# Attention stage of a three-layer kernel: causal blocks cut in half, 64 by 64 tiles, two tile forms per pair

## The chip, the cores and the metric

One Trainium2 chip, one core. The metric is the device time of one execution in microseconds. The median of three runs of the kernel before is 829.82 us (828.93 to 831.88).

## What is computed

A retention layer (attention without softmax, with a causal decay) on 4 batches of 8 heads, 576 positions, head size 64, and behind it two dense layers with a hidden width of 2,048 on 2,304 tokens of width 512.

```python
scores = scale * np.matmul(q, k.transpose(0, 1, 3, 2))
gamma = 1.0 - 2.0 ** (-5.0 - np.arange(H, dtype=np.float32))
rel = pos[:, None] - pos[None, :]
Dmat = np.where(rel >= 0, gamma[:, None, None] ** rel[None, :, :], 0.0)
x = np.matmul(scores * Dmat, v)              # then heads side by side: 2304 x 512
h = x @ w_in;  x = (np.maximum(h, 0.0) + alpha * np.minimum(h, 0.0)) @ w_out
h = x @ w_in2; x = (h / (1.0 + np.exp(-1.702 * h))) @ w_out2
```

## The kernel before

The kernel has three stages: the attention, the first dense layer (`mm1`, `mm2`, L391 to L467) and the second one (`unit1`, `unit2`). Only the attention is touched.

It works on 16 pairs of heads (4 batches times 4 pairs). The 576 positions are cut into four chunks of 128 and one of 64. The decay over a distance is split into a factor per key, a factor per query and a power per chunk, so that a chunk needs three things: `a_scores` multiplies keys and queries of the same chunk (128 by 128), `a_outer` makes one 64 by 64 state per chunk from keys and values, which ACT scales out of PSUM (`a_states`) and DVE sums up over chunks (`a_sums`), and `a_values` adds the values of the own chunk (weights `v`, moving the masked scores `r`) to the product of the queries with the summed state. The last chunk of 64 has a state tail of its own. `a_evac` takes the scores out of PSUM and multiplies them by a table of mask and key factors (`diag_sb`, built by ACT in `a_tables`); `a_out` multiplies the result by the query factors (`otab_sb`) into `xs`; `xa_split` writes it as a rounded part (ACT) and a rest (DVE), which the first dense layer reads.

All of it is fp32. The two heads of a pair lie on the two halves of the 128 partitions, so scores use tiles of 64 rows by 128 columns, the states 128 by 64, the product with the state 64 by 64.

The order of instructions is written out by hand: every engine runs its instructions in the order in which the program issues them. The loop over `i` (L712 to L734) issues for turn `i` the scores, key scaling and evacuation of pair `i`, its states and sums, then the values and output of pair `i - 1`, then the load of pair `i + 3`. Conversion steps of the first three weight chunks (`w_load` to `w_lo`) and the splits stand in a list with due times in turns; `run_to` issues those that are due, at the turn's begin, at 0.25 and at 0.75. Loads of pairs and of these weights are all issued by SP, in order. `tmp` gives a pair's load one of four buffers, so a load waits until the values four pairs earlier have been computed. PSUM holds two buffers of scores (two banks each), one of states and one of values.

Of the kernel before, what the change touches and what calls it, by code (L numbers as in the profile page):

```python
# [21 lines left out]
LAG = 2  # L22
F64_MIN = 2.0 ** -15
F64_MAX = 2.0 ** 17 * (1 - 2.0 ** -24)
TMP = {"ld": (4, 5, 6, 7), "r": (8, 9), "xs": (10, 11, 12, 13, 14, 15)}
# [14 lines left out]
def kernel(  # L40
# [29 lines left out]
    vtab_sb = att.tile([128, NP, 5], F32, name="vtab_sb")  # L70
    mask_sb = att.tile([128, 192], F32, name="mask_sb")
    diag_sb = att.tile([128, NP, 2, 1, 128], F32, name="diag_sb")
    tail_sb = att.tile([128, NP, 64], F32, name="tail_sb")
    otab_sb = att.tile([128, NP, S], F32, name="otab_sb")
# [156 lines left out]
    def a_load(i):  # L231
        b, p = PAIRS[i]
        t = tmp("ld", i, [128, 1728])
        if i == 0:
            nc.sync.dma_start(out=t[:, 0:512], in_=qkv[b, p, :, 0:512])
            nc.sync.dma_start(out=mask_sb, in_=mask)
            nc.sync.dma_start(out=vtab_sb, in_=vtab)
            nc.sync.dma_start(out=t[:, 512:1152], in_=qkv[b, p, :, 512:1152])
            nc.sync.dma_start(out=kts[:, 0], in_=kn[b, p])
            nc.sync.dma_start(out=t[:, 1152:1728], in_=qkv[b, p, :, 1152:1728])  # L240
        else:
            nc.sync.dma_start(out=t, in_=qkv[b, p])
            nc.sync.dma_start(out=kts[:, i % 4], in_=kn[b, p])
        if i == 1:
            nc.sync.dma_start(out=otab_sb[:, :, 0:128], in_=otab)
        q = [t[:, j * 128:j * 128 + 128] for j in (0, 1, 4, 5)] + [t[:, 768:832]]
        k = [t[:, j:j + 128] for j in (256, 384, 832, 960)] + [t[:, 1088:1152]]
        ld[i] = q, k, t[:, 1152:1728].rearrange("p (n d) -> p n d", n=9)

    def scale(out, in_, by):  # L250
        nc.scalar.activation(out=out, in_=in_, func=ACTF.Copy, scale=by)

    def a_tables(p):
        for e in range(2):
            scale(diag_sb[:, p, e, 0], mask_sb[:, 0:128], vtab_sb[:, p, e:e + 1])
        scale(tail_sb[:, p], mask_sb[:, 128:192], vtab_sb[:, p, 2:3])

    def a_otab(p):
        o = otab_sb[:, p]
        for n in (128, 256):  # L260
            copy(o[:, n:2 * n], o[:, 0:n])
        copy(o[:, 512:S], o[:, 0:S - 512])

    def mm(out, lhsT, rhs, start, stop):
        nc.tensor.matmul(out=out, lhsT=lhsT, rhs=rhs, start=start, stop=stop, skip_group_check=True)  # L265

    halves = (slice(0, 64), slice(64, 128))

    def a_keys(i):
        n = kts[:, i % 4].rearrange("p (j n) -> p j n", j=4)  # L270
        for e, o in enumerate(halves):
            scale(n[:, :, o], n[:, :, o], vtab_sb[:, PAIRS[i][1], e:e + 1])
        k_t[i] = n

    def a_scores(i):
        q, k = ld[i][0:2]
        t = aps.tile([128, 2, 512], F32, tag="sc", name="sc", bufs=2)
# [5 lines left out]
    def a_outer(i):  # L283
        q, k, v = ld[i]
        t = s_t[i] = aps.tile([128, 512], F32, tag="st", name="st")
        for o in halves:
            mm(t[o, 0:64], k[4][o], q[4][o], True, True)
        n = k_t.pop(i)
        for j in range(4):
# [3 lines left out]
    def a_evac(i):  # L293
        r = tmp("r", i, [128, 1600])
        r_t[i] = (
            r[:, 0:1024].rearrange("p (e n) -> p e n", e=2), r[:, 1024:1536],
            r[:, 1088:1600].rearrange("p (b n) -> p b n", b=2)[:, :, 0:64],
        )
        nc.vector.tensor_tensor(
            out=r[:, 0:1024].rearrange("p (e j n) -> p e j n", e=2, j=4),  # L300
            in0=sc_t.pop(i).rearrange("p e (j n) -> p e j n", j=4),
            in1=diag_sb[:, PAIRS[i][1]].to_broadcast([128, 2, 4, 128]), op=ALU.mult,
        )


    def a_states(i):
        p = PAIRS[i][1]
        s = r_t[i][1]
        scale(s[:, 0:320], s_t.pop(i)[:, 0:320], vtab_sb[:, p, 3:4])

    def a_sums(i):
# [3 lines left out]
            out=s[:, 320:512], in0=s[:, 64:256], scalar=vtab_sb[:, p, 3:4], in1=s[:, 128:320],  # L315
            op0=ALU.mult, op1=ALU.add,
        )
        half = r_t[i][2]
        nc.vector.scalar_tensor_tensor(
            out=s[:, 384:512].rearrange("p (b n) -> p b n", b=2), in0=half,  # L320
            scalar=vtab_sb[:, p, 4:5], in1=s[:, 384:512].rearrange("p (b n) -> p b n", b=2),
            op0=ALU.mult, op1=ALU.add,
        )
        nc.vector.tensor_tensor(out=s[:, 0:64], in0=s[:, 0:64], in1=tail_sb[:, p], op=ALU.mult)

    def a_values(i):
        q, _, v = ld[i]
        r, s = r_t.pop(i)[0:2]
        t = av_t[i] = aps.tile([128, 1024], F32, tag="av", name="av")
        out = [t[:, A0 + j * 128:A0 + j * 128 + 128] for j in range(4)] + [t[:, A0 + 512:A0 + S]]  # L330
        for c in range(1, 5):
            s0 = 64 if c == 1 else 192 + c * 64
            for o in halves:
                mm(out[c][o], s[o, s0:s0 + 64], q[c][o], c < 3, False)
        for o in halves:
# [577 lines left out]
```

## Time and profile before

| what | value |
|---|---|
| median of three runs | 829.82 us |
| the profiled execution | 827.3 us |
| its span, first to last instruction | 825.5 us |
| TensorE busy, granted clock | 99% of the span, 1.00 |
| VectorE, ScalarE, GpSimd busy | 77%, 56%, 2% |
| DMA over the span | 202 GB/s |

PE stands for TensorE, DVE for VectorE, ACT for ScalarE, POOL for GpSimd, SP for SyncE; PEld are TensorE's weight loads. "L265" is line 265 of the kernel. Since all fp32 products of the attention go through the helper `mm`, they have one line, L265, and are told apart by the tiles they write and read: `sc` scores, `st` states, `av` values. Each call of `mm` shows as two MATMUL rows. The rows on which the prediction rests stand in a section of their own below.

### The profile page before, as it was taken

To read this page: it belongs to the slowest core of one execution; us is meant where nothing else is said; L and a number is where in the kernel's file an instruction comes from. 1 tells how busy PE (TensorE), PEld (TensorE's weight loads), DVE (VectorE), ACT (ScalarE), POOL (GpSimd) and SP (SyncE) were. 2 spreads that over 40 slices of the span, in tenths; PEclk is the share of its full clock that TensorE was granted. 3 is DMA by queue.
4 is the path that set the end of the run, shared out by engine and by line. 5 is a ranking of instruction groups with operands and counts; after the bars stand their busy time and mean duration, and the time that the engine had idled before them with its cause. 6 is when DMAs were issued, how large, how long until landed. Compare 5 with 4: busy or idle time off the path is not lost.

```text
span 825.5 us, 13947 instructions
## 1 busy us (share of the span) xinstructions
PE 816.9 (99%) x5114; PEld 745.9 (90%) x5114; DVE 633.6 (77%) x1128; ACT 460.0 (56%) x920; POOL 17.9 (2%) x36
## 2 busy tenths in 40 slices
PE   8999999999999999999999999999999999999998
PEld 7888888888888888998888899999999999999998
DVE  4898886787575678668668787789777799677875
ACT  5644664555343544564445676666566666566653
POOL 0000000000001010000010000000000000000000
PEclk9999999999999999999999999999999999999999
DMA  8995743445174575665564654787543986446871
GB/s 313 340 351 193 254 153 103 147 160 179 51 255 161 187 227 168 203 210 147 191 208 134 212 170 135 265 298 260 179 133 114 366 291 231 137 133 201 295 266 73
DMA packets 66100, 166.97 MB, mean 202 GB/s; under 512 B 7152, under 2 KB 33392, under 8 KB 60272
## 3 DMA queue, kind: packets, MB, share of 16 engines
q1 hardware_dynamic: 61424, 149.30, 53.1%
q0 software_dynamic: 4608, 16.78, 6.9%
q8 instruction: 40, 0.66, 0.3%
q14 instruction: 28, 0.23, 0.1%
HBM read 128.83 MB, written 37.22 MB: 201 GB/s over the span
## 4 chain that ended last, share of the span: by engine, by line
PE 89%; DMA 4%; DVE 4%; SPq 1%; issue 1%; ACT 1%; ACTq 0%; DVEq 0%
PE acc L561 24%; PE h L397 20%; PE acc L440 19%; PE h L561 18%; PE av L265 4%; DMA ld<-in_qkv_dram 2%; PE sc L265 2%; PE st L265 1%; DMA rg<-sums 1%; DMA rw<-rg 1%; DVE x L88 1%; SPq L205 1%; DVE gsf L88 1%; DMA sg<-sums 0%; DVE cv L137 0%
## 5 line engine op out<-in xcount | busy, mean ns | idle before, releaser
L440 PE MATMUL acc<-gsf,w 128*128 128x512 f32 (+1 forms) x960 | 210.9, 368 | 1.3 <-ACT gsf L85 0.9
L397 PE MATMUL h<-x,w 128*128 128x512 f32 (+1 forms) x960 | 210.3, 368 | 0.0
L440 PEld LDWEIGHTS acc<-gsf,w 128*128 128x128 f32 x960 | 168.2, 188 | 32.5 <-DVE gsf L88 1.3
L85 ACT ACTIVATE gsf<-g 128x384 fp32r<-128x384 f32 (+2 forms) x248 | 133.6, 544 | 113.0 <-DVE g L409 66.0
L397 PEld LDWEIGHTS h<-x,w 128*128 128x128 f32 x960 | 168.2, 189 | 30.5 <-DVE w L88 0.4
L88 DVE TENSOR_TENSOR gsf<-g,gsf 128x384 fp32r<-128x384 f32 (+2 forms) x248 | 141.8, 580 | 52.5 <-ACT gsf L85 51.9
L561 PE MATMUL acc<-x,ws 128*128 128x384 f32 x552 | 106.8, 334 | 0.0
L409 DVE SCALAR_TENSOR_TENSOR g<-h,nalpha_sb,g 128x512 f32<-128x512 f32 (+1 forms) x80 | 55.6, 695 | 66.5 <-ACT h L408 66.2
L561 PE MATMUL acc<-gsf,ws 128*128 128x384 f32 x576 | 101.3, 334 | 0.0
L561 PEld LDWEIGHTS acc<-gsf,ws 128*128 128x128 f32 x576 | 100.0, 188 | 0.0
L561 PEld LDWEIGHTS acc<-x,ws 128*128 128x128 f32 x552 | 96.7, 188 | 0.0
L561 PE MATMUL h<-x,ws 128*128 128x384 f32 x456 | 90.6, 334 | 0.2 <-DVE x L88 0.2
L407 ACT ACTIVATE g<-h 128x512 f32<-128x512 f32 (+1 forms) x80 | 43.9, 549 | 72.5 <-PE h L397 72.4
L561 PEld LDWEIGHTS h<-x,ws 128*128 128x128 f32 x456 | 80.1, 188 | 0.6 <-DVE x L88 0.6
L561 PE MATMUL h<-gsf,ws 128*128 128x384 f32 x432 | 76.3, 334 | 0.0
L561 PEld LDWEIGHTS h<-gsf,ws 128*128 128x128 f32 x432 | 75.0, 188 | 0.0
L468 DVE TENSOR_TENSOR tm<-h,tm 128x384 f32<-128x384 f32 x73 | 40.5, 555 | 31.7 <-PE h L561 27.5
L88 DVE TENSOR_TENSOR ws<-rw,ws 128x512 fp32r<-128x512 f32 x96 | 57.1, 616 | 0.6 <-ACT ws L85 0.6
L468 DVE TENSOR_TENSOR g<-g,g 128x384 f32<-128x384 f32 x93 | 51.5, 554 | 0.7
L85 ACT ACTIVATE ws<-rw 128x512 fp32r<-128x512 f32 x96 | 50.0, 569 | 0.4 <-DMA rw<-rg 0.4
L408 ACT ACTIVATE h<-h 128x512 f32<-128x512 f32 (+1 forms) x80 | 43.9, 549 | 0.0
L116 ACT ACTIVATE cv<-raw 128x1024 f32<-128x1024 f32 x32 | 36.2, 1131 | 7.2 <-DMA raw<-in_w_dram 5.1
(73 smaller groups left out, 695.4 us busy)
## 6 DMA issues: line engine op xcount, KB each, us to landing
ws<-sg SPq DMA_DIRECT2D x42, 1024.0 KB, 6.4
raw<-in_w_dram SPq DMA_DIRECT2D x32, 512.0 KB, 5.0
raw<-in_w_dram POOLq DMA_DIRECT2D x32, 512.0 KB, 5.0
ld<-in_qkv_dram SPq DMA_DIRECT2D x15, 864.0 KB, 6.7
rw<-rg SPq DMA_DIRECT2D x24, 512.0 KB, 3.5
rw<-rg SPq DMA_DIRECT2D x24, 384.0 KB, 3.1
sg<-sums SPq DMA_DIRECT2D x40, 128.0 KB, 2.1
kts<-in_kn_dram SPq DMA_DIRECT2D x16, 256.0 KB, 6.9
```

What stands on the lines that cost most here:

```text
L85: return nc.scalar.activation(out=out, in_=in_, func=ACTF.Copy)
L88: return eng.tensor_tensor(out=out, in0=a, in1=b.bitcast(F32), op=ALU.subtract)
L116: nc.scalar.activation(out=cvs[key], in_=raws[key][:, :, 1].bitcast(F32), func=ACTF.Abs)
L205: nc.sync.dma_start(out=dst[:, c], in_=t)
L265: nc.tensor.matmul(out=out, lhsT=lhsT, rhs=rhs, start=start, stop=stop, skip_group_check=True)
L397: nc.tensor.matmul(out=t, lhsT=w[:, cw, k * 128:k * 128 + 128], rhs=x[:, cx], start=(i == 0), stop=(i == 3 * NK - 1),)
L407: nc.scalar.activation(out=g, in_=t, func=ACTF.Relu)
L408: nc.scalar.activation(out=t, in_=t, func=ACTF.Relu, scale=-1.0)
L409: nc.vector.scalar_tensor_tensor(out=g, in0=t, scalar=nalpha_sb[:, m:m + 1], in1=g, op0=ALU.mult, op1=ALU.add)
L440: nc.tensor.matmul(out=acc[0][d], lhsT=w[:, cw, d * 128:d * 128 + 128], rhs=g[:, cx], start=(m == m0 and i == 0), stop=(m == m1 - 1 and i ...
L468: nc.vector.tensor_tensor(out=out, in0=x, in1=y, op=op)
L561: nc.tensor.matmul(out=out, lhsT=w(cw), rhs=x(cx), start=(start and n == 0), stop=True, skip_group_check=True,)
```

## The change

Chunks are 128, 128, 128 and 192 positions now. A chunk's block of scores is cut in halves of 64: second-half queries with all keys of the chunk, and a corner of first-half queries with first-half keys. All scores are computed with tiles of 64 rows and 64 columns, on all four such tiles of the array; the corners of two chunks share the four tiles, for which keys and values of some chunks are stored with their halves swapped. The values fall into three groups: `a_corners` and `a_across` in 64 by 64 tiles, `a_within` in 128 by 64. In a turn PE does scores and corners (64 by 64), states and within (128 by 64), across (64 by 64, as the scores that follow). `a_across` gets an added dependency: its first product waits for ACT's copy of the states of the pair behind. There are three states per pair instead of four, so `kn` has 384 columns instead of 512.

PSUM: scores in three single banks, one bank of states, two buffers of values. Loads: five buffers (tile `w10` joins), issued up to four pairs ahead; the first three pairs are loaded in pieces. Pair 0 is finished within turn 0, and turn 1 has no values. Tables are built by DVE (pairs 0 and 1) and POOL (2 and 3); the split's subtraction and the tail product go to POOL; the output table has 192 columns and is used by two instructions. Weight steps have other due times.

```diff
-TMP = {"ld": (4, 5, 6, 7), "r": (8, 9), ...
+TMP = {"ld": (4, 5, 6, 7, 4, 5, 6, 10, 7, 4, 5, 6, 10, 7, 4, 5), "r": (8, 9), ...
     def a_load(i):
+        cuts = {0: (0, 512, 1152, 1728), 1: (0, 1152, 1728), 2: (0, 1152, 1728)}.get(i, (0, 1728))
+        for n, (c0, c1) in enumerate(zip(cuts, cuts[1:])):
+            nc.sync.dma_start(out=t[:, c0:c1], in_=qkv[b, p, :, c0:c1])
+            if i == n == 0:
+                nc.sync.dma_start(out=vtab_sb, in_=vtab)
+                nc.sync.dma_start(out=mask_sb[:, 3], in_=mask)
+            if n == 0:
+                nc.sync.dma_start(out=kts[:, i % 5], in_=kn[b, p])
...
     def a_keys(i):
         for e, o in enumerate(halves):
-            scale(n[:, :, o], n[:, :, o], vtab_sb[:, PAIRS[i][1], e:e + 1])
+            for j, c in ((slice(0, 2), 4 * e), (slice(2, 3), 3 * e + 1 - e)):
+                scale(n[:, j, o], n[:, j, o], vtab_sb[:, PAIRS[i][1], c:c + 1])
     def a_scores(i):
-        for j in range(4):
-            for e, o in enumerate(halves):
-                mm(t[:, e, j * 128:j * 128 + 128], k[j][o], q[j][o], j == 0, True)
+        for c in range(4):
+            n = slice(c * 64, c * 64 + 64 + c // 3 * 64)
+            for h in halves:
+                for e, o in enumerate(halves):
+                    mm(t[e][h, n], k[c][o, h], q[c][o, 64:], c == 0, True)
+        for c in (0, 2, 1, 3):
+            for e, o in enumerate(halves):
+                h, n = first(e, c), 320 + c % 2 * 64
+                mm(t[e][h, n:n + 64], k[c][o, h], q[c][o, 0:64], False, True)
...
     def a_evac(i):
+        for e, t in enumerate(sc_t.pop(i)):
+            nc.vector.tensor_tensor(
+                out=r_t[i][0][:, e], in0=t[:, 0:448], in1=diag_sb[:, PAIRS[i][1], e], op=ALU.mult
+            )
     def a_sums(i):
...
-        nc.vector.tensor_tensor(out=s[:, 0:64], in0=s[:, 0:64], in1=tail_sb[:, p], op=ALU.mult)
+        nc.gpsimd.tensor_tensor(out=s[:, 0:64], in0=s[:, 0:64], in1=tail_sb[:, p], op=ALU.mult)
+    def a_corners(i):
+        for c in (0, 2, 1, 3):
+            for e in (0, 1) if c < 2 else (1, 0):
+                h, n = first(e, c), 320 + c % 2 * 64
+                done[0] = mm(
+                    av_t[i][1][c][halves[e], 0:64], v[h, 2 * c + e], r[h, e, n:n + 64], c % 2 == 0, True
+                )
+    def a_within(i):
+        for c in range(4):
+            for e, o in enumerate(halves):
+                mm(
+                    av_t[i][1][c][o, 64:], v[:, 2 * c + e], r[:, e, c * 64:c * 64 + 64 + c // 3 * 64],
+                    False, True,
+                )
+    def a_across(i, behind):
+        for c, n in ((2, 256), (3, 320), (4, 0), (1, 64)):
             for o in halves:
+                if c == 4:
+                    ins = mm(av_t[i][1][3][o, 128:192], v[o, 8], s[o, 0:64], False, True)
+                else:
+                    ins = mm(av_t[i][1][c][o], s[o, n:n + 64], q[c][o], False, True)
+                if behind is not None:
+                    tc.add_manual_dep(ins.ins, behind.ins.name, SYNC, reason="row tiles of one bank")
+                    behind = None
     def a_out(i):
+        for c0, c1, n in ((0, 384, 128), (384, S, 192)):
...
     def xa_split(i, c):
-        sub(nc.vector, x[:, 1], f, x[:, 0])
+        sub(nc.gpsimd, x[:, 1], f, x[:, 0])
...
     rows = (
-        (1.8, 7.0, 7.75, 8.75, 9.75, 10.25, 10.75), (7.2, 11.0, 11.75, 12.75, 13.75, 14.25, 14.75),
-        (11.0, 14.75, 15.6, 16.0, 16.25, 16.5, 16.6),
+        (2.8, 5.25, 5.75, 6.75, 7.75, 8.25, 9.25), (6.8, 9.5, 10.25, 11.75, 12.75, 13.25, 14.25),
+        (10.6, 14.25, 15.0, 15.75, 16.0, 16.25, 16.6),
     )
...
         for i in range(n_a + 1):
             if i < n_a:
                 a_scores(i)
+                if i == 0:
+                    a_tables(0)
+                    a_tables(2)
                 a_keys(i)
                 a_evac(i)
             run_to(i)
+            j = max(i - 1, 0)
+            if i != 1:
+                a_corners(j)
             if i < n_a:
                 a_outer(i)
-                a_states(i)
+                behind = a_states(i)
                 a_sums(i)
...
             run_to(i + 0.25)
-            if i:
-                a_values(i - 1)
-                a_out(i - 1)
-            else:
-                fill(5)
-            if i + 3 < n_a:
-                a_load(i + 3)
+            if i != 1:
+                a_within(j)
+                a_across(j, behind)
+                a_out(j)
+            for n in {0: (3, 4), 1: (), 4: (7, 8)}.get(i, (i + 3 + (i > 4),)):
+                if n < n_a:
+                    a_load(n)
             run_to(i + 0.75)
```

## Rows read from the trace of the kernel before

**Rows 1.** The page, busy time of the first engines.

```profile
PE 816.9 (99%) x5114; PEld 745.9 (90%) x5114; DVE 633.6 (77%) x1128; ACT 460.0 (56%) x920; POOL 17.9 (2%) x36
```

**Rows 2.** PE's timeline, one pair: start us, length us, engine, line, operation.

```profile
30.70 1.16 PE L265 MATMUL sc<-ld 64*128 64x128 f32 x16
31.79 0.33 PE L265 MATMUL st<-ld 64*64 64x64 f32 x4
32.05 0.69 PE L265 MATMUL st<-ld,kts 128*64 128x64 f32 x16
32.67 0.99 PE L265 MATMUL av<-ld,r 64*64 64x128 f32 x16
33.49 1.31 PE L265 MATMUL av<-r,ld 64*64 64x64 f32 x20
34.73 0.38 PE L265 MATMUL sc<-ld 64*128 64x128 f32 x2
```

**Rows 3.** PE's timeline, the scores of the first three pairs.

```profile
4.76 1.96 PE L265 MATMUL sc<-ld 64*128 64x128 f32 x16
...
10.40 1.16 PE L265 MATMUL sc<-ld 64*128 64x128 f32 x16 [0.77 <-DMA ld<-in_qkv_dram]
...
14.60 0.60 PE L265 MATMUL sc<-ld 64*128 64x128 f32 x6
```

**Rows 4.** The timeline, end of the attention stage.

```profile
72.54 0.99 PE L265 MATMUL av<-ld,r 64*64 64x128 f32 x16 [0.95 <-DVE xs L344]
...
74.59 1.67 PE L397 MATMUL h<-x,w 128*128 128x512 f32 x6
```

**Rows 5.** Windows: stretch, its length, busy us (instructions), clock, DMA share, GB/s.

```profile
10.00:15.00 5.00, 4.60 (x78) 4.14 (x80) 2.36 (x5) 3.23 (x10) 0.00 (x0) 1.00 1.07 421
...
40.00:45.00 5.00, 5.00 (x96) 4.37 (x96) 4.93 (x10) 1.87 (x5) 0.00 (x0) 1.00 0.92 289
...
10.00:66.00 56.00, 55.44 (x984) 48.69 (x986) 49.31 (x87) 32.02 (x76) 0.00 (x0) 1.00 0.96 350
66.00:76.00 10.00, 9.05 (x142) 7.79 (x139) 9.50 (x15) 3.33 (x6) 0.00 (x0) 1.00 0.33 108
```

**Rows 6.** DMA issues until 66 us: size each, median us to landing.

```profile
ld<-in_qkv_dram SPq DMA_DIRECT2D x15, 864.0 KB, 6.7
kts<-in_kn_dram SPq DMA_DIRECT2D x16, 256.0 KB, 6.9
```

**Rows 7.** SP's own waits until 76 us: total, times, longest.

```profile
SPq L242 <- PE av L265: 33.5, 12, 4.4
```

**Rows 8.** The chain of waits in order of time, around the eleventh pair.

```profile
38.86 8.13 DMA ld<-in_qkv_dram
```

**Rows 9.** DVE's timeline, one pair with the clamps of a weight chunk.

```profile
53.82 1.22 DVE L299 TENSOR_TENSOR r<-sc,diag_sb 128x1024 f32<-128x1024 f32 x1
54.96 0.41 DVE L314 SCALAR_TENSOR_TENSOR r<-r,vtab_sb 128x192 f32<-128x192 f32 x1
...
55.80 0.75 DVE L344 TENSOR_TENSOR xs<-av,otab_sb 128x576 f32<-128x576 f32 x1
56.47 0.69 DVE L120 TENSOR_SCALAR cv<-cv 128x1024 f32<-128x1024 f32 x1
...
57.80 1.22 DVE L299 TENSOR_TENSOR r<-sc,diag_sb 128x1024 f32<-128x1024 f32 x1
```

**Rows 10.** Groups by line until 90 us: count, busy us, mean ns, idle before.

```profile
L251 ACT ACTIVATE kts<-kts,vtab_sb 128x256 f32<-128x256 f32 x32 | 14.4, 498 | 5.0 <-DMA kts<-in_kn_dram 4.8
L251 ACT ACTIVATE r<-st,vtab_sb 128x320 f32<-128x320 f32 x16 | 8.4, 527 | 19.5 <-PE st L265 12.4 <-issue 7.1
L88 DVE TENSOR_TENSOR x<-xs,x 128x512 fp32r<-128x512 f32 x4 | 2.7, 682 | 0.0
L88 DVE TENSOR_TENSOR x<-xs,x 128x448 fp32r<-128x448 f32 x4 | 2.5, 615 | 0.0
L88 DVE TENSOR_TENSOR x<-xs,x 128x64 fp32r<-128x64 f32 x4 | 0.9, 215 | 0.0
```

More of the change, by code (lines that the diff above doesn't have):

```diff
@@ L258, in a_otab @@
     def a_otab(p):
[L259 to L262, printed above, removed]
+        o = otab_sb[:, p, 0]
+        scale(o[:, 128:192], o[:, 0:64], vtab_sb[:, p, 7:8])
     def mm(out, lhsT, rhs, start, stop):
-        nc.tensor.matmul(out=out, lhsT=lhsT, rhs=rhs, start=start, stop=stop, skip_group_check=True)
-    halves = (slice(0, 64), slice(64, 128))
+        return nc.tensor.matmul(
+            out=out, lhsT=lhsT, rhs=rhs, start=start, stop=stop, skip_group_check=True
+        )
@@ L322, in a_sums @@
             op0=ALU.mult, op1=ALU.add,
         )
-        nc.vector.tensor_tensor(out=s[:, 0:64], in0=s[:, 0:64], in1=tail_sb[:, p], op=ALU.mult)
-    def a_values(i):
-        q, _, v = ld[i]
[L328 to L332, printed above, removed]
-            for o in halves:
-                mm(out[c][o], s[o, s0:s0 + 64], q[c][o], c < 3, False)
-        for o in halves:
-            mm(out[4][o], v[o, 8], s[o, 0:64], False, True)
-        for j in range(4):
-            for e, o in enumerate(halves):
-                mm(out[j][o], v[:, 2 * j + e], r[:, e, j * 128:j * 128 + 128], False, True)
+        nc.gpsimd.tensor_tensor(out=s[:, 0:64], in0=s[:, 0:64], in1=tail_sb[:, p], op=ALU.mult)
@@ new lines, in a_corners @@
+    def a_corners(i):
+        v, r = ld[i][2], r_t[i][0]
+        t = aps.tile([128, 1024], F32, tag="av", name="av", bufs=2)
+        av_t[i] = t, [t[:, A0 + c * 128:A0 + c * 128 + 128 + c // 3 * 64] for c in range(4)]
+        for c in (0, 2, 1, 3):
[3 more added lines that the diff above has]
+                    av_t[i][1][c][halves[e], 0:64], v[h, 2 * c + e], r[h, e, n:n + 64], c % 2 == 0, True
+                )
@@ L699 @@
     with tc.manual_schedule():
-        kts = wp.tile([128, 4, 512], F32, tag="w3", name="kts")
+        kts = wp.tile([128, 5, 384], F32, tag="w3", name="kts")
         nc.vector.memset(wz, 0.0)
-        wps = aps.tile([128, 2, 512], F32, tag="sc", name="wps", bufs=2)
+        wps = aps.tile([128, 512], F32, tag="sc", name="wps", bufs=3)
         def fill(n):
             for i in range(n):
-                nc.tensor.matmul(out=wps[:, 0, 0:128], lhsT=wz, rhs=wz, start=True, stop=True)
+                nc.tensor.matmul(out=wps[:, 0:128], lhsT=wz, rhs=wz, start=True, stop=True)
         fill(8)
+        copy(wz, wz)
+        done = [None]
         for i in range(3):
@@ L711 @@
         nc.sync.dma_start(out=alpha_sb, in_=alpha)
+        a_masks()
         for i in range(n_a + 1):
@@ L719 @@
             run_to(i)
+            j = max(i - 1, 0)
+            if i != 1:
+                a_corners(j)
             if i < n_a:
                 a_outer(i)
-                a_states(i)
+                behind = a_states(i)
                 a_sums(i)
-            run_to(i + 0.25)
-            if i:
-                if i <= NP:
-                    a_otab(i - 1)
-                a_values(i - 1)
-                a_out(i - 1)
-            else:
-                fill(5)
-            if i + 3 < n_a:
-                a_load(i + 3)
+            else:
+                behind = copy(wz[:, 0:1], wz[:, 0:1])
+                tc.add_manual_dep(behind.ins, done[0].ins.name, SYNC, reason="row tiles of one bank")
+            if i < NP:
+                a_otab(i)
+            if i == 0:
+                a_tables(1)
+                a_tables(3)
+            run_to(i + 0.25)
+            if i != 1:
[5 more added lines that the diff above has]
+                    a_load(n)
             run_to(i + 0.75)
@@ L863, in _layout @@
     d = {}
+    order = np.arange(S)
+    swap = [np.concatenate([order[c:c + 64] + 64, order[c:c + 64]]) for c in (0, 128, 256, 384)]
+    keep = [order[c:c + 128] for c in (0, 128, 256, 384)]
+    heads = [
+        np.concatenate(t + [order[512:]]) for t in (keep[:2] + swap[2:], swap[:2] + keep[2:])
+    ]
+    k, v = (
+        np.stack([t[:, h][:, heads[h % 2]] for h in range(H)], axis=1) for t in (k, v)
+    )
     qt = q.transpose(0, 1, 3, 2).reshape(B, NP, 128, S)
```

119 lines of the change are left out of this document (60 added, 59 removed).

## The prediction

> **What bounds the kernel now.** The page first: TensorE (PE) is busy for 99% of the span [rows 1], so only what moves PE's work, or makes it wait, can move the end. The change touches one stage alone, the attention, which runs from the start until the first matmul of the dense layers at 74.59 us [rows 4]; the other 751 us of the 825.5 us span keep their instructions.
>
> Then PE's timeline of one pair of heads in the middle of that stage [rows 2]. It goes through five groups: scores from 30.70, state tail from 31.79, states from 32.05, values from 32.67 (two groups, across and within, which one row joins), and at 34.73 the next scores: 4.03 us a pair, no idle time in the rows. A fp32 `mm` call is two MATMUL rows (8 calls are x16), I call each a pass, and every group has two 64-wide tiles of the array working side by side. The state tail is 2 passes of 64 columns per tile in 0.26 us, the states are 8 in 0.62: six more passes cost 0.36, so a pass of 64 is 0.06 and a change of form 0.14. The two value groups have 14 passes of 128 and 4 of 64 per tile and two changes in 2.06 us: (2.06 - 0.24 - 0.28) / 14 = 0.11 for a pass of 128. One of 192 is then 0.16. Every fifth of a pair's time goes into changes of form.
>
> Then the loads. From 10 to 66 us the DMA engines show a busy share of 0.96 while they move 350 GB/s [rows 5]; in stretches of 5 us they give 421 at best and 289 at worst. A pair's load takes 6.7 us from issue to landing [rows 6]. SP's waits say that it mostly held loads back for PE to free a buffer, 33.5 us in 12 times [rows 7]; but the chain of waits shows one load of 8.13 us that PE then waited for [rows 8]. So the loads are a second limit close under PE's.
>
> Last VectorE (DVE): a pair without other work takes it from evacuation to the end of the output product 1.14 + 0.84 + 0.67 = 2.65 us, by the starts in its timeline; the clamps of the weight conversion add 1.33 [rows 9], and it is late at the end of the stage, where PE waits 0.95 us for an output product [rows 4].
>
> **The change, part by part.**
> *PE's groups.* Two forms are left, so three changes go. In the form 64 by 64 a diagonal tile now does: across 128, 192, 64 and 128 columns, 2 x (0.11 + 0.16 + 0.06 + 0.11) = 0.88; scores, 6 passes of 64 and 2 of 128, 0.58; corners of the scores 4 x 0.06 = 0.24; tail 0.12; corners of the values 0.24. That is 2.06, and the two tiles off the diagonal have less (1.06), if all four run side by side. In the form 128 by 64: states 0.36, within 0.58. With two changes of 0.14 to 0.2 a pair is 2.06 + 0.94 + 0.30 = 3.30 us, 0.73 less. No row of before has four tiles at once: a pass in all four costs 0.06 as for two, or 0.12 if two pairs take turns. I take 0.06, since two row halves (scores) and two column halves (states) each overlap in rows 2; the other end is a rival.
>
> *The start.* The first pair is now finished in its own turn. Before: scores at 4.76, the second pair's at 10.40 after a wait for its load, the third's at 14.60 [rows 3]. Now the second piece of the first load stands behind the keys on SP, so first scores end near 7.2; evacuation 1.1, corners and change 0.4, states 0.4, ScalarE (ACT) 0.5 + 0.2, sums 0.6, across 0.9 give 11.4; the second pair's scores and states add 1.6: the third pair's scores start at 13.1. Bounds: 12.0, if the second pair's scores need not wait for the first pair's sums that long, and 14.6 as before. The five fill matmuls that go were no work; SP issues 15 loads for 12, hidden behind the bytes in flight, and without that cover three more issues.
>
> *The end.* After the last pair's 3.3 us PE has corners, within, across and three changes: 0.24 + 0.58 + 0.88 + 0.43 = 2.1. The wait for the output product goes: its bank has a second buffer.
>
> *The loads.* The keys shrink from 256 to 192 KB; 15 pairs of 864 + 192 KB and three weight chunks of 1,024 KB, plus tables, are 19.6 MB after the first pair's landing at about 6.3 us (its scores end at 6.7, [rows 3]). Buffers go from four to five and a load is issued a pair earlier, so SP holds back less. The rate then sets the landing of the last pair: 350 GB/s [rows 5], the mean of before with its holding back, gives 62.3 us; 421 gives 52.9, earlier than PE can use. I take 365, near the mean because the share was already 0.96: 6.3 + 53.7 = 60.0. PE alone would reach these scores at 13.1 + 13 x 3.30 = 56.0. So the loads become the limit by 4 us, and the stage ends at 60.0 + 3.3 + 2.1 = 65.4. The seventh load waits on SP for a split on GpSimd (POOL) and holds the eighth and a weight piece behind it; both were issued four pairs ahead, which covers it, and without that cover it is up to one turn, 3.3 us.
>
> *DVE.* Evacuation in two pieces of 448: 1.14 for 1,024 against 0.67 for 576 is 1.05 ns a column and 0.07 a piece [rows 9], so 1.07; output product in two, 0.74; sums without the tail product, 0.6. 2.41 a pair. Weight pieces add 1.33 or 1.14 in ten of the turns 5 to 15: 3.5 a turn there against PE's 3.3. It reaches the last sums at 23.0 + 36.6 + 1.0 = 60.6, earlier than PE needs them when the loads pace it (62.5). The tables of the first two pairs move from ACT to DVE, ahead of its first evacuation.
>
> *ACT and the new wait.* The across group now waits for ACT's state copy of the pair behind it. That copy takes 0.53 for 320 columns [rows 10], so about 0.47 for 256; between states and across PE has 0.58 + 0.14 of its own, which covers it. Queued behind the waiting matmul are across and all later scores. If ACT is late by a weight step (six lie in the stage, of 1,024 columns, so over 1 us by the 0.53 for 320) the cover is gone, at 0.5 to 0.9 each; with 4 us of waiting for loads around it I count nothing, and 2 us at worst. Keys in four pieces instead of two of 0.50 [rows 10] add about 0.2 to ACT, which has room.
>
> *POOL.* The x subtractions, four each of 512, 448 and 64 columns, are 2.7 + 2.5 + 0.9 = 6.1 us on DVE [rows 10]. POOL shows nothing at all in the windows [rows 5], so its price is open: 6.1 from below, twice that from above; off the path either way, as the dense layers read the results later. What it could do to DVE is a rival.
>
> The sum against the profiled execution: 74.59 - 65.4 = 9.2 us off a span of 825.5, so 827.3 becomes 818.1. The median of the three runs is 829.82, 2.5 above that execution; the same 9.2 off it is **820.6 us**.
>
> **The rivals.**
> *Loads no limit.* If the longer queue moves 400 GB/s or more, as in the best stretch [rows 5], PE paces: 56.0 + 3.3 + 2.1 = 61.4, a gain of 13.2, 816.6 us. Against it: the mean was 350 at nearly a full share.
> *Starts too dense.* Matmul starts in the states group are 0.03 us apart on average, the tightest in rows 2. If that is a floor between 0.015 and 0.03, a pass in four tiles costs 0.06 to 0.12. Half-way, 0.09: 6 passes of scores and 8 of corners cost 0.42 more, 3.72 a pair; third pair at 13.4, last scores at 61.8, end 67.7, gain 6.9: 822.9 us. The Trainium skill, "TensorE: Matmul & The Clock Gate", section "Wait — 56ns, not 53.3ns?", says that starts never come closer than about 25 ns; by it a pass in four tiles would be 0.10, and the time by this estimate about 825. No row of before shows or excludes it.
> *Two tiles at a time: slower.* At 0.12 the 64 by 64 form holds 0.88 + 1.16 + 0.48 + 0.12 + 0.48 + 0.14 = 3.26, and a pair takes 4.36, more than the 4.03 of before: third pair at 13.9, last scores at 70.6, end at 77.3, 2.7 us later than now: 832.5 us. It decides from 4.2 us a pair on. For it: no four tiles in the trace. Against it: both kinds of neighbours overlap.
> *POOL stops DVE.* If DVE stands still while POOL subtracts, at POOL's upper price it loses 12.2 us, less some 2.7 of idle time in turns 2 to 4: last sums at 70.1, end at 71.1, gain 3.5: 826.3 us. For it speaks that DVE has little slack. The Trainium skill, "SBUF — State Buffer", section "SBUF: two separate sides", has it that a DVE instruction with two SBUF inputs and a POOL instruction that reads SBUF exclude each other for their whole length. No run here shows it; evacuation and output product read PSUM and would not be touched, so I price it as the upper case.
> *The gain does not arrive.* Weight chunks of the dense layers could be late instead; 829. Against it: DMA share 0.33 in the stage's last 10 us leaves room [rows 5].
>
> **How the numbers follow.** Forecast 48%; loads no limit 15%; starts too dense 10%; two at a time 9%; POOL stops DVE 12%; no gain 6%. The forecast's own bounds are 818 (380 GB/s) to 824.5 (350 GB/s and 2 us of ACT). The range takes in the first three and most of the POOL case, 815.5 to 827.0, and leaves out two at a time, no gain and a little more: 18%. About 0.3%, 2.5 us, is what a measurement of this kernel can tell from no change: faster than that 82%, within it 12% (no gain, part of POOL and of two at a time), slower 6%.
>
> **What would show it.** PE's timeline: a pair in two forms, with about 3.3 us of work and a wait of the scores for the load in most later turns; scores of pair 2 near 13 us; first dense matmul near 65. Four tiles: the scores group, 0.94 with corners and tail, near 1.0, not 1.8. DMA: 360 to 370 GB/s from 10 to 60 us. DVE's sums: no gaps as long as POOL's subtractions. Wrong would be: PE pairs of 3.7 or more without a load's wait, across waiting for ACT in most turns, or a granted clock below 1.00 in the first 12 us, where PE has gaps of over 1 us.

## The result, and the profile after

The changed kernel takes 836.58 us (median of 5 runs, 835.13 to 838.18), the kernel before beside it 828.99 (5 runs, 827.83 to 831.88): a ratio of 1.0086, interval 1.0061 to 1.0111. The forecast was 820.6 us, a gain, in a range of 815.5 to 827.0; it is a loss of 7.6 us, outside that range.

TensorE's busy time fell by 3 us against [rows 1], though its instructions rose by 630 in each of the two kinds. From the page of the kernel after, PE's line and the line of the instruction queue:

```profile
PE 814.0 (97%) x5744; PEld 742.6 (89%) x5744; DVE 636.0 (76%) x1153; ACT 455.7 (54%) x934; POOL 40.3 (5%) x82
...
q8 instruction: 45, 0.74, 0.4%
```

The stage itself, PE's timeline of one pair that nothing disturbs (the fourth), of the next pair's beginning and of the end (answering [rows 2] and [rows 4]):

```profile
19.61 1.25 PE L286 MATMUL sc<-ld 64*64 64x64 f32 x43
...
20.76 0.41 PE L286 MATMUL av<-r,ld 64*64 64x64 f32 x15
21.10 0.57 PE L286 MATMUL st<-ld,kts 128*64 128x64 f32 x12
21.50 0.74 PE L286 MATMUL av<-r,ld 128*64 128x64 f32 x16
22.32 0.76 PE L286 MATMUL av<-ld,r 64*64 64x128 f32 x8
...
23.14 1.07 PE L286 MATMUL sc<-ld 64*64 64x64 f32 x45
...
24.16 0.28 PE L286 MATMUL av<-r,ld 64*64 64x64 f32 x5
26.92 0.50 PE L286 MATMUL av<-r,ld 64*64 64x64 f32 x9 [2.48 <-issue]
...
84.19 6.19 PE L442 MATMUL h<-x,w 128*128 128x512 f32 x26
```

This pair takes 3.53 us (19.61 to 23.14), near the 3.30 of the sum and well under the 4.03 of before. But the first dense matmul comes at 84.19, not at 65.4 and not at the 74.59 of [rows 4]: 9.6 us later than before (the dense layers add 1.3 us, 752.2 against 750.9, which I can't explain). The two profiled executions are 10.9 us apart, more than the medians: that of before lies 1.7 us under its median, that of after 1.6 over. The row at 26.92 shows why the stage is late: in the middle of the corner products PE stands still for 2.48 us, and the releaser is "issue", which means that no semaphore held it. The longest of PE's waits from 5 to 90 us (total, times, longest):

```profile
PE av L286 <- issue: 7.2, 3, 2.5
PE sc L286 <- issue: 2.1, 1, 2.1
PE st L286 <- issue: 2.0, 1, 2.0
PE sc L286 <- DVE r L327: 1.1, 1, 1.1
PE sc L286 <- DMA ld<-in_qkv_dram: 0.7, 1, 0.7
```

Five such stops, 11.3 us; the kernel before has none. The real waits, for DVE and for loads, are small. Two further views tell what the stops are. First the windows from one stop to the next; the bracketed numbers behind PE and PEld are the instructions:

```profile
26.90:39.20 12.30, 9.79 (x254) 8.34 (x253) 9.38 (x16) 7.46 (x21) 5.25 (x8) 0.86 0.85 326
39.20:55.20 16.00, 13.71 (x380) 12.11 (x381) 12.87 (x24) 7.29 (x17) 3.33 (x6) 0.89 0.88 307
55.20:65.30 10.10, 7.75 (x254) 6.76 (x254) 8.48 (x17) 3.96 (x14) 1.69 (x3) 1.00 0.81 296
65.30:71.60 6.30, 3.78 (x127) 3.28 (x127) 4.00 (x8) 1.53 (x5) 0.32 (x1) 0.98 0.62 228
```

Matmuls and weight loads together are 507, 761, 508 and 254: multiples of 254, or one short of one (the single records add PE's own semaphore waits, which makes it 512, 768, 512 and 256). Then the DMA queues during the stop from 36.90 to 39.20:

```profile
q1 hardware_dynamic: 264, 0.93, 101.0%
q8 instruction: 1, 0.02, 2.6%
```

One packet of the instruction queue runs in it, beside data queues that fill the DMA engines. (In the last stop the data queues are light, 24.4% from 69.20 to 71.60 us, but its packet had started 4.1 us after the multiple of 256 that is spoken of below.) The page counts 45 such packets with 0.74 MB, 16 KB each, or 64 bytes for each of 256 instructions. The other pages keep that ratio to the matmuls and weight loads: 40 packets for 10,228 in before, 44 for 11,252 in bsplit, 43 for 10,976 in merge. My theory F from this: PE's program is itself loaded in packets of 256 instructions, a packet is asked for when the one before is begun, and under the pair loads it comes late. When it is asked for is part of the theory; the rest can be seen. By the single records of the trace, from 15 to 75 us a packet started 1.6 to 4.4 us after PE had crossed a multiple of 256 (3.4 to 4.4 at the five stops) and took 0.95; PE resumed 1.2 to 1.5 us after its end. Before, 144 instructions a pair of 4.03 us use up a packet in 7.2 us; after, 224 in 3.53 us do so in 4.0. The cover was gone: if the boundaries of before lie at the same counts as those of after, its packets too started 0.5 to 3.4 us late, and had landed 2.8 us or more ahead of need.

The windows show what follows from a stop:

```profile
24.45:26.90 2.45, 0.00 (x0) 0.00 (x0) 1.05 (x2) 0.00 (x0) 0.20 (x1) 1.00 1.00 328
26.90:30.35 3.45, 3.43 (x45) 2.83 (x46) 1.42 (x2) 1.96 (x7) 1.21 (x2) 0.51 0.93 369
...
10.00:66.00 56.00, 45.05 (x1302) 39.15 (x1302) 43.76 (x87) 27.12 (x79) 17.83 (x33) 0.94 0.86 311
```

While PE stands in this stop, the granted clock still reads 1.00; as it resumes it is 0.51, the 1.2 GHz level, and full again 3.45 us later. Two more such stretches of 3.4 us lie at two of the other four stops: one begins at 40.58, 1.3 us after PE had resumed, one at 71.30, just before it did. In stretches of 5 us the clock reads 0.69 (25 to 30), 0.66 (40 to 45) and 0.66 (70 to 75), so 1.55 + 1.7 + 1.7 = 5 us of full-speed work. Against 1.00, 0.96 and 350 GB/s in [rows 5], the last row above has clock 0.94, DMA share 0.86, 311 GB/s: the loads were not the limit.

### The profile page after: what moved, and what is told of

It is laid out like the page before. It is cut to its first block, busy times and chain, and to the rows that moved or that the text cites. A ratio compares the mean times of both kernels' runs of the same rounds, so it can differ in the third digit from the quotient of the medians.

```text
span 836.4 us, 15331 instructions
## 1 busy us (share of the span) xinstructions
PE 814.0 (97%) x5744; PEld 742.6 (89%) x5744; DVE 636.0 (76%) x1153; ACT 455.7 (54%) x934; POOL 40.3 (5%) x82
## 4 chain that ended last, share of the span: by engine, by line
PE 77%; DVE 9%; DMA 5%; issue 5%; ACT 4%; SPq 0%; POOL 0%; DVEq 0%; ACTq 0%
PE acc L606 23%; PE h L606 18%; PE h L442 16%; PE acc L485 15%; DMA rg<-sums 3%; PE av L286 2%; DVE cv L131 1%; DVE gsf L89 1%; DVE sums L513 1%; DVE cv L138 1%; PE st L286 1%; DMA rw<-rg 1%; PE sc L286 1%; DVE g L454 1%; DMA sg<-sums 1%
## 5 line engine op out<-in xcount | busy, mean ns | idle before, releaser
L452 ACT ACTIVATE g<-h 128x512 f32<-128x512 f32 (+1 forms) x80 | 43.8, 547 | 69.8 <-PE h L442 69.7
```

The lines of the kernel that those rows point to most:

```text
L452: nc.scalar.activation(out=g, in_=t, func=ACTF.Relu)
```

## The experiments

All runs, from their profiled execution: first dense matmul, stops with releaser "issue" until 95 us (number), granted clock from 15 to 70 us; and the median.

| kernel | dense from | stops | clock | median us |
|---|---|---|---|---|
| before | 74.6 | 0 | 1.00 | 828.8 to 829.2 |
| after | 84.2 | 11.3 (5) | 0.94 | 836.58 |
| noload | 69.8 | 2.1 (1) | 1.00 | 822.96 |
| half | 73.3 | 2.4 (3) | 0.97 | 826.62, one run |
| shift | 94.8 | 9.6 (6) | 0.94 | 847.86, one run |
| pieces | 83.4 | 12.1 (8) | 0.97 | 836.34 |
| spread | 83.7 | 9.6 (5) | 0.94 | 833.93 |
| merge | 76.2 | 4.0 (5) | 0.97 | 831.12 |
| bsplit | 88.4 | 0 | 1.00 | 842.72 |
| start | 85.4 | 14.1 (10) | 0.97 | 838.45 |
| sync | 85.3 | 12.1 (7) | 0.91 | 840.92 |
| subdve | 84.0 | 11.6 (6) | 0.94 | 838.56 |
| mspread | 74.6 | 4.5 (4) | 1.00 | 829.18 |
| mstart | 77.6 | 6.7 (4) | 0.94 | 829.41 |
| best1 | 76.7 | 5.7 (6) | 0.94 | 828.45 |
| bests | 71.8 | 4.1 (3) | 1.00 | 826.68 |

A profile is one execution, so a stage end may stand some way off the median: the profiled execution of spread is 2.4 us over its median, the slowest of its runs, and that of bests 2.8 under, the fastest. Medians can be set beside each other, since the kernel before was measured with each of them, at 828.8 to 829.2 us.

**noload**, the pair loads taken away:

```diff
     def a_load(i):
         b, p = PAIRS[i]
+        if i >= 4:
+            ld[i] = kept[i % 4]
+            return
...
```

> The changed kernel in which pairs 4 to 15 load nothing: each takes the tiles that pair i mod 4 loaded, so q, k and v of those pairs are left out of the computation. Theory F (the five stops of TensorE are its own instruction stream: after every 256 of its instructions a packet of 16,384 bytes is needed, and it stands behind the pair loads): with no loads in flight no stop over 0.5 us after 20 us, a pair of 3.4 to 3.5 us, granted clock 1.00 from 13 us on, first dense matmul at 68 to 71 us instead of 84.2, whole time 820 to 824 us. Rival R (the stops come from the attention itself: the two tile forms, a bank, a semaphore): five stops of 2.1 to 2.5 us at 24, 37, 53, 63 and 69 us stay, first dense matmul 82 to 85 us, whole time 834 to 838 us.

822.96 us, ratio 0.9922 (0.9896 to 0.9948) to before. One stop is left, which theory F had not expected; it lies where the last of the first four loads had just been under way (DMA share 1.02 from 15 to 20 us, 0.30 from 20 to 25). Then 1,159 matmul rows run at clock 1.00 and DMA share 0.15, and by the records the packets there start at most 1.2 us after a boundary. Timeline, and two windows:

```profile
22.73 0.27 PE L292 MATMUL sc<-ld 64*64 64x64 f32 x2 [2.06 <-issue]
...
69.83 0.50 PE L448 MATMUL h<-x,w 128*128 128x512 f32 x1
```
```profile
10.00:15.00 5.00, 4.92 (x92) 4.30 (x92) 3.86 (x12) 1.77 (x6) 3.51 (x10) 0.50 1.05 404
26.34:62.60 36.26, 35.27 (x1159) 31.26 (x1152) 35.38 (x72) 22.70 (x63) 12.40 (x20) 1.00 0.15 47
```

So the same instructions, forms and banks run without a stop when no loads compete: rival R falls. It also splits the loss: of the 14.4 us between the two stage ends (84.2 - 69.8), 9.2 are stops (11.3 - 2.1) and 5.0 the half clock beside them.

**shift**, 128 instructions ahead of the attention:

```diff
-                nc.tensor.matmul(out=wps[:, 0:128], lhsT=wz, rhs=wz, start=True, stop=True)
-        fill(8)
+                nc.tensor.matmul(out=wps[:, 0:32], lhsT=wz, rhs=wz[:, 0:32], start=True, stop=True)
+        fill(40)
```

> The changed kernel with the 8 fills of 128 columns at the start made 40 fills of 32 columns: as long on TensorE, but 128 instructions more in its stream ahead of the attention (4 a fill). Theory F: the stops come 128 instructions earlier in a pair's work, about 2.0 us of it (128 of the 224 rows of a 3.5-us pair): the first one starts near 22.4 us instead of 24.45, and between the first rows after two stops there are again a multiple of 256 instructions; whole time within 2 us of 836.6. Rival R: the stops start where they do now, at 24.45, 36.94, 53.2, 62.3 and 69.2 us within 0.5 us, at the same matmul of a pair.

The time misses both expectations and is no test: a fill row of 32 columns took 0.22 us (4.67 us for 21 rows, and the weight loads are busy for 17.14 of the 17.20 us of the fills), nearly the 0.23 of one of 128 columns, so the first scores came at 18.26 instead of 4.77. The places are one. Counted from the first scores to a stop, windows of the kernel after, then of shift:

```profile
4.70:26.85 22.15, 16.95 (x460) 14.40 (x460) 17.07 (x42) 9.78 (x33) 10.85 (x26) 1.00 0.89 319
4.70:39.20 34.50, 26.74 (x714) 22.74 (x713) 26.45 (x58) 17.25 (x54) 16.09 (x34) 0.95 0.88 322
```
```profile
18.24:40.70 22.46, 19.35 (x523) 16.73 (x523) 16.61 (x37) 11.97 (x40) 9.45 (x20) 1.00 0.47 170
18.24:46.60 28.36, 23.22 (x650) 20.12 (x650) 21.12 (x45) 15.32 (x48) 11.36 (x23) 1.00 0.59 216
```

After: 460 and 714 matmul rows, 79 over a multiple of 127. Shift: 523 and 650, 15 over one. The stops came 64 rows (and as many weight loads) sooner in the attention's work, and 64 matmul rows had been put ahead. The stops belong to the place in PE's stream, not to a place in a pair.

**pieces and spread**, other forms of the loads: each load of pairs 5 to 15 in three parts, issued together (pieces), or each behind a group of TensorE (spread, the second line of the diff, which stands behind the other groups too).

```diff
+            queue.extend([(t[:, n:n + 576], qkv[b, p, :, n:n + 576]) for n in (0, 576, 1152)])
...
                 a_outer(i)
+                issue(per, last[0])
```

> The changed kernel with the load of 864 KB of pairs 5 to 15 cut into three and all pieces issued at once where the load was: the number of transfers doubles, the bytes that wait ahead of an instruction packet stay. Theory F: stops as before, 835 to 839 us. A theory of large single transfers (one DMA of 864 KB blocks the rings) expects stops of under 1 us and 826 to 830 us.

> The same pieces, each issued only when the scores, the outer products, the within products or the across products of the turn are done, so that at most one or two pieces wait ahead of an instruction packet. Theory F: the stops shrink to under 1.2 us each, the granted clock falls less often, first dense matmul 74 to 79 us, whole time 826 to 831 us. Rival R: five stops as now, 834 to 839 us. A third way: the late pieces arrive too late and TensorE waits for ld instead, 836 to 842 us with waits for DMA ld in the rows.

836.34 and 833.93 us. The size of a transfer is not it: pieces stayed where theory F had it. Issuing behind the groups gave 2.4 us, less than half of what theory F expected (826 to 831); with five stops of 9.6 us spread lies at the edge of rival R's 834 to 839. Packets still started up to 4.5 us after their boundary, by their records, while fresh pieces went on being issued. So what delays a packet is not only what was queued when it was asked for; how the chip orders the two queues stays open.

**half**, half of a pair's tile and no keys: 432 KB instead of 864 + 192 (442 and 1,081 thousand bytes):

```diff
+        if i >= 4:
+            ld[i] = kept[i % 4]
+            nc.sync.dma_start(out=raw[i % 4][:, 0:864], in_=qkv[b, p, :, 0:864])
+            return
```

> The changed kernel in which pairs 4 to 15 load only the first 864 columns of their tile (442 KB instead of 1081 KB a pair) into the tiles of pairs 0 to 3 and take the rest from these, so that part of q, k and v of those pairs is left out. Theory F with the bytes under way as the measure: the packet starts 1 to 2.5 us after its boundary instead of 2.8 on the mean, most stops vanish and the rest are under 1 us, 823 to 827 us. If any load in flight at all makes the packet late: stops of 2 us stay at four or more boundaries, 830 to 836 us.

826.62 us in one run, as theory F had it with the bytes under way as the measure; three stops of 1.0 us or less (and one wait of 2.4 us for a late load):

```profile
PE av L293 <- issue: 1.4, 2, 0.9
PE st L293 <- issue: 1.0, 1, 1.0
```

So with less than half of a pair's traffic the stops are fewer and shorter, though a load is issued for every pair. It is one run, and by the records one packet still started 4.9 us after its boundary, in the stretch of that late load; the amount of traffic matters, but that it alone sets a packet's delay is not shown.

**merge**, fewer instructions for the same columns. A corner of the scores uses the weights of a diagonal product, so the two become one call; the columns of `diag_sb` and `r` are put in another order for it.

```diff
-        for c in (0, 2, 1, 3):
-            for e, o in enumerate(halves):
-                h, n = first(e, c), 320 + c % 2 * 64
-                mm(t[e][h, n:n + 64], k[c][o, h], q[c][o, 0:64], False, True)
...
+                    if h != first(e, c):
+                        out, rhs = out[:, 1:], rhs[:, 1:]
+                    mm(out, k[c][o, h], rhs, c == 0, True)
```

> The changed kernel with the 8 corner products of the scores made part of the 16 score products that use the same weights (128 or 192 columns instead of 64 or 128): the same columns, but 48 instead of 56 calls, 192 instead of 224 rows of matmul and weight load a pair. Theory F (256 instructions are a packet, and under load the next packet comes 5.7 to 6.7 us after the last boundary was crossed): 256 rows last about 4.6 us instead of 4.0, 12 boundaries in the stage instead of 14, all stops together 7 to 9 us instead of 12.4, whole time 830 to 833 us. Rival (TensorE's stops come from the amount of work or of loads, not from the number of instructions): 835 to 838 us.

831.12 us, 5.5 under after, ratio 1.0028 (1.0006 to 1.0049). Two of its rows of waits:

```profile
PE sc L286 <- issue: 3.1, 3, 1.2
PE st L286 <- issue: 0.9, 2, 0.5
```

Five stops again, but 4.0 us in place of 11.3, less than expected (the 12.4 of the expectation counts a wait of 1.07 us for DVE among after's stops): 32 instructions a pair fewer gave most of the loss back. A pair that nothing disturbs took 3.37 us (22.83 to 26.20), so that 256 instructions lasted 4.5 us. That is the number of instructions at work, beside unchanged loads.

**bsplit**, the other way round in the kernel before:

```diff
-        for j in range(4):
+        for j in range(8):
             for e, o in enumerate(halves):
-                mm(t[:, e, j * 128:j * 128 + 128], k[j][o], q[j][o], j == 0, True)
+                mm(t[:, e, j * 64:j * 64 + 64], k[j // 2][o], q[j // 2][o, j % 2 * 64:j % 2 * 64 + 64], j == 0, True)
```

> The kernel before, its own tiles and order, with each score product and each value product of 128 columns cut into two of 64: the same result, 208 instead of 144 rows of matmul and weight load a pair. By the rows a call of 64 costs 0.06 and one of 128 0.11, so the cut itself costs about 0.1 us a pair, 2 us in all. Theory F: the boundaries come every 5 us instead of 7.1, under the 5.7 to 6.7 us of a packet under load, so stops with no releaser of 0.5 to 1.7 us appear where the kernel before has none, and the whole time is 833 to 838 us. Rival (the number of instructions doesn't matter): 830 to 832 us and no such stops.

842.72 us and no stop at all: both expectations are wrong in time, and it decides nothing between them. The reason is in its scores:

```profile
40.98 2.00 PE L265 MATMUL sc<-ld 64*128 64x64 f32 x32
42.91 0.33 PE L265 MATMUL st<-ld 64*64 64x64 f32 x4
...
45.90 2.00 PE L265 MATMUL sc<-ld 64*128 64x64 f32 x32
```

In the form 64 by 128 a pass of 64 columns cost nearly as much as one of 128 (1.93 us for 32 rows to the tail at 42.91, against 1.09 for 16 in [rows 2]). A pair became 4.92 us long, so 256 instructions of 208 a pair lasted 6.1 us, and with that a packet was in time. Theory F allows this, and so does its rival; the run was meant to go under the bound of 5.7 to 6.7 us and did not.

**start and sync**, two ways to make PE quicker without touching packets or loads:

```diff
-        eng = nc.gpsimd if p > 1 else nc.vector
+        eng = (nc.vector, nc.scalar, nc.scalar, nc.gpsimd)[p]
...
```
```diff
-                behind = a_states(i)
+            behind = copy(wz[:, 0:1], wz[:, 0:1])
+            tc.add_manual_dep(behind.ins, done[0].ins.name, SYNC, reason="row tiles of one bank")
...
```

> The changed kernel with the tables of the first pairs spread out: those of pairs 1 and 2 built by ACT, those of pair 0 by DVE alone, those of pair 3 by POOL; one fill more at the start and three between the scores and the corners of the first pair. Theory: scores of the third pair at 13 to 14 us instead of 16.27, no first table operation over 0.35 us on DVE, granted clock 1.00 from 8 us or earlier. If that gain stays: 831 to 833.5 us. If the instruction packets take it back, since the boundaries then come while more loads are under way: 834.5 to 837 us.

> The changed kernel in which the across products wait for a small ACT copy behind the corners instead of for ACT's copy of the states (the state copy is then 13 waits of 4.1 us in all less on the path). If the wait is simply added to the stops: 831.5 to 833.5 us. Theory F: the boundaries only come sooner and the stops grow by what is saved: 834.5 to 837 us, with stops of 14 to 16 us in all.

838.45 us (837.79 to 839.16) and 840.92 us (835.45 to 841.49), 1.9 and 4.3 slower than after by the medians, beyond what even theory F gave; one of sync's four runs lies within after's range. In start the third pair's scores do come 1.5 us sooner, though not at 13 to 14 us (they now wait 0.70 for their load),

```profile
14.75 1.03 PE L292 MATMUL sc<-ld 64*64 64x64 f32 x48 [0.70 <-DMA ld<-in_qkv_dram]
```

but there are ten stops of 14.1 us. In sync the stops are 12.1 us and the clock from 15 to 70 us is 0.91. That a saving is taken back was expected; that it costs more than it saves I had not, and why it does is only partly seen: more stops in one, more half clock in the other.

**subdve**, the subtraction of x on DVE as before:

```diff
-        sub(nc.gpsimd, x[:, 1], f, x[:, 0])
+        sub(nc.vector, x[:, 1], f, x[:, 0])
```

> The changed kernel with the subtraction of the split of x back on DVE instead of POOL, so that POOL does not hold DVE up in the middle of the stage. Theory F (the stops decide): 834.5 to 838 us, DVE's scalar_tensor_tensor of 128x64 never over 0.4 us beside it. If DVE's wait for POOL were what slowed the stage: 830 to 833.5 us. If the subtraction makes DVE the limit: 838.5 to 842 us.

838.56 us (837.42 to 839.56), half a microsecond over the first expectation and just inside the third, between which it does not decide, with 11.6 us of stops as in after; the second falls. POOL does hold DVE up, as the rows of after (DVE, POOL) and of this run (DVE) show, but taking that away made nothing faster:

```profile
29.44 1.36 DVE L342 SCALAR_TENSOR_TENSOR r<-r,vtab_sb 128x64 f32<-128x64 f32 x1
...
29.46 1.55 POOL L89 TENSOR_TENSOR x<-xs,x 128x512 fp32r<-128x512 f32 x2 [0.20 <-ACT x L86]
```
```profile
29.28 0.28 DVE L342 SCALAR_TENSOR_TENSOR r<-r,vtab_sb 128x64 f32<-128x64 f32 x1
```

**mspread, mstart, best1 and bests**, the edits put together on merge (best1: with start and sync; bests: with spread too).

> The merged scores together with the loads of pairs 5 to 15 cut into pieces and issued behind TensorE's groups. By the two runs before (merged scores -5.5 us, pieces issued behind the groups -2.4 us against pieces issued at once) 828 to 830 us if both add, with all stops together under 3.5 us instead of 5.4. If the place of the loads doesn't matter: 830.5 to 833 us and stops of 5 to 6 us.

> The merged scores together with the spread-out tables and the added fills of the start. In the changed kernel these made the third pair start 2 to 3 us sooner and the whole 2 us slower, since the stops grew. With 192 rows a pair theory F expects less of that: stops of 5 to 7 us, 828 to 831 us. If a sooner start is always taken back by the instruction packets: 831 to 834 us.

> Merged scores, the start as in the run before, and the across products waiting for a small copy behind the corners instead of for the copy of the states. If TensorE's own pace decides now: 1 to 3 us under the run before, 826 to 829 us. Theory F (a quicker pair meets the next packet sooner): within 1.5 us of the run before or above it, with stops of 7 us or more.

> All four edits: merged scores, the start spread out, the small copy behind the corners, and the loads of pairs 5 to 15 in pieces issued behind TensorE's groups. The first three together stand at 828.45 us, 0.7 under the kernel before; the pieces took 2.4 us off the changed kernel and 1.9 off the merged one. If that adds: 826 to 827.5 us, a ratio to the kernel before of 0.996 to 0.998. If the stops that remain only move: 828 to 830 us.

829.18, 829.41, 828.45 and 826.68 us, each within the time that its first expectation or theory F gave; best1 lies within both of its expectations and decides nothing. With 192 instructions a pair the start and the small copy no longer harm, and spread gives 1 to 2 us again, though in mspread not through shorter stops (4.5 us against the 3.5 that was expected; merge has 4.0 in the table, not the 5.4 of that expectation). Only all four together are clear of the kernel before: 0.9976 of it (0.9961 to 0.9991). Its window and two of its waits:

```profile
10.00:66.00 56.00, 48.10 (x1316) 42.16 (x1318) 46.45 (x93) 36.74 (x113) 19.44 (x36) 1.00 0.97 350
```
```profile
PE av L303 <- issue: 3.1, 2, 2.2
PE sc L303 <- DMA ld<-in_qkv_dram: 2.9, 4, 1.8
```

The clock is full, the DMA share 0.97, and waits for loads stand beside the 4.1 us of stops that are left: the loads have become the next limit, as the prediction had it for the change itself.

## Why the prediction was wrong

The step that failed is the one from PE's groups to the end of the stage: the sum priced an instruction by its columns and its form, and had no term for bringing the instructions themselves, nor for the half clock beside the stops; the runs show 11.3 us of stops and 5 us of half clock there. A second term was mis-sized, the start (13.1 for 16.27 us). The sum had the count in hand: in [rows 5] the 1,970 matmuls and weight loads of 56 us are 256 in 7.3 us, and the calls that the change adds (56 for 36 a pair) make 256 last 4.0. What a packet costs under load the kernel before did not show as a wait, since 7.2 us covered it. So a price that is hidden by a cover came to 11 us without one, and the instruction stream was not among the things whose cover the prediction looked for.

Point by point, against 84.2 for a stage end of 65.4:

- *PE's groups.* 3.30 forecast, 3.53 after; in noload 3.52 on the mean of the last 13 pairs without the stop, and 3.39 where it is shortest (53.84 to 57.23). The mechanism was right, four tiles at once included: scores with corners take 1.02 us in noload (46.92 to 47.94, rows below), where two tiles at a time would be 1.64. So "two tiles at a time" (4.36 a pair) falls, and so does "starts too dense" (3.72) as a pair. Its premise was half right: those 1.02 us are 0.82 in the sum, and leave 0.08 for a pass of 64 in four tiles, between the sum's 0.06 and the rival's 0.09. The across group made up for it, 0.71 against 0.88 (49.73 to 50.44). The 0.2 over is mostly the wait for ACT, below: without that wait, in sync, a pair that nothing disturbs took 3.25 us (65.08 to 68.33). 13 pairs make 2.8 us.
- *The start.* 13.1 forecast, 16.27 measured, outside its bounds of 12.0 to 14.6: +3.2. DVE built the tables of two pairs while POOL built two others, at 0.43 us an operation, against 0.29 alone in start (DVE's groups of after and of start), and the second set stood ahead of the evacuation that the third pair's scores waited for (after's DVE and PE):

```profile
L268 DVE TENSOR_TENSOR diag_sb<-mask_sb,vtab_sb 128x128 f32<-128x128 f32 x12 | 4.7, 431 | 0.0
L274 DVE TENSOR_TENSOR diag_sb<-mask_sb,vtab_sb 128x128 f32<-128x128 f32 x6 | 1.5, 288 | 0.0
```
```profile
10.32 1.28 PE L286 MATMUL av<-r,ld 128*64 128x64 f32 x16
...
11.88 2.93 DVE L268 TENSOR_TENSOR diag_sb<-mask_sb,vtab_sb 128x128 f32<-128x128 f32 x8
...
16.27 0.96 PE L286 MATMUL sc<-ld 64*64 64x64 f32 x43 [1.07 <-DVE r L327]
...
17.97 0.74 PE L286 MATMUL av<-r,ld 128*64 128x64 f32 x16
```

  The sum had named the move and given it no price. PE also seems to have run at half clock there: 16 rows of the within group took 1.28 us at 10.32 and 0.74 at 17.97, and in noload, with the same durations, the granted clock reads 0.50 from 10 to 15 us (after's own trace holds no clock reading before 13.3 us, and its windows print 1.00). The prediction had listed this as a sign of being wrong. How much of the 3.2 us each of the two costs no run separates.
- *The loads.* The forecast let them set the pace at 365 GB/s, 4.0 us behind PE. PE waited 0.7 us for a piece of the first and for none after it; the term was not paid. Even without stops it would not have been: from 16.27, 13 pairs of 3.53 end at 62.2, after the 60.0 of the loads.
- *These three and the one stop of noload* give 2.8 + 3.2 - 4.0 + 2.1 = 4.1 of the 4.4 us between 65.4 and noload's 69.8; the rest is the end, 5.8 us from the last pair's scores for 5.4. Of the other 14.4 us stops are 9.2 and half clock 5.0: no term of the sum at all.
- *ACT and the new wait.* Taken as covered, 2 us at worst; it was 4.1 us in 13 waits of up to 0.3, by the weight loads' waits in after:

```profile
PEld av L286 <- ACT r L251: 4.1, 13, 0.3
```

  But sync, which takes it away, was not faster (840.92 us): under the stops it was not the limit.
- *POOL.* 5.1 + 4.6 + 1.3 = 11.0 us for the subtractions of x, within 6.1 to 12.2, near the upper end. That POOL stops DVE is true (1.36 us for 0.28), but it did not pace the stage: subdve is no faster. The Trainium skill, "SBUF — State Buffer", section "SBUF: two separate sides", says that a DVE instruction with two SBUF inputs and a GpSimd instruction that reads SBUF exclude each other; these rows agree.
- *DVE.* 3.5 us a turn with weight pieces was right: in noload it is busy for 35.38 of 36.26 us, with pairs of 3.5 us on the mean, so even without stops it had next to no room for a faster PE there.
- *The sign.* "Slower" had 6%. By its time "two tiles at a time" (832.5) came nearest and by its kind "the gain does not arrive" (829), both for reasons that have no part in it: four tiles did work at once, and PE's rows show no wait for a weight chunk.
- *The bounds.* Worked out again, the forecast's own bounds are 818.5 and 824.9 where it says 818 and 824.5; nothing hangs on it.

## What to carry to other kernels

Count instructions, not only their time: here 256 matmuls and weight loads (with TensorE's own semaphore waits) were one packet of 16 KB, safe beside the loads when they lasted 6 to 7 us (bsplit, before), late by 0.4 to 1.2 us when they lasted 4.5 (merge), and stopping TensorE for 2 us and more when they lasted 4 (after). A wait with releaser "issue" in the middle of a group, at a distance of a multiple of 256 instructions, is the sign of it; calls that share weights and could be joined were the best single cure here (5.5 us). And when a change removes time from an engine, ask for each thing that the old time covered, the engine's own program among them.

## What the hardware showed that I had not expected

- A stop can cost more than its own length: at three of after's five stops, those of 2.3 to 2.5 us, the granted clock read the 1.2 GHz level for some 3.4 us at their end or soon after, which costs 1.7 us of full-speed work.
- Cutting passes shorter did not make them cheaper in the form 64 by 128: 32 rows of 64 columns took 1.93 us, 60 ns each, and 16 rows of 128 took 1.09, 68 ns each. In the form 64 by 64, on four tiles, rows of mostly 64 columns come much closer. By noload's rows,

```profile
46.92 0.27 PE L292 MATMUL sc<-ld 64*64 64x64 f32 x1
...
47.94 0.23 PE L292 MATMUL st<-ld 64*64 64x64 f32 x2
...
50.44 0.27 PE L292 MATMUL sc<-ld 64*64 64x64 f32 x1
```

  48 score rows start within 1.02 us, 21 ns apart on the mean. The Trainium skill, "TensorE: Matmul & The Clock Gate", section "Wait — 56ns, not 53.3ns?", has 25 ns as the least distance; with four tiles side by side the measured mean is below it, and the estimate of 0.10 us a pass that the prediction works out from that figure was too dear (0.08 measured).
